# Sliding-window attention and a max-out feed-forward on one core: scores in 64x64 tiles for half of the chunks, masks as a minimum, and every slot written out by hand

## The chip, the cores and the metric

The kernel runs on one core of one Trainium2 chip. The metric is the device time of one execution in microseconds (us); lower is better. A profiled execution gives a page and a trace, in which each engine's instructions stand with their start and their duration: PE is TensorE's matmul, PEld its weight load, DVE VectorE, ACT ScalarE, POOL GpSimd, and SP the engine whose queue issues most of the DMAs.

## The reference

```python
# q, k, v: [4 batches, 8 heads, 768 positions, 64], float32; n_sink = 4, window = 128
scores = (q @ k.transpose(0, 1, 3, 2)) / 8
rel = pos[:, None] - pos[None, :]
keep = (pos[None, :] < n_sink) | ((rel >= 0) & (rel < window))
a = softmax(where(keep, scores, -1e9))
x = (a @ v).transpose(0, 2, 1, 3).reshape(3072, 512)
h = maximum(maximum(x @ w1, x @ w2), x @ w3)      # 512 -> 768
out = h @ w_out                                   # 768 -> 512
```

Each query sees the 128 keys up to its own position, and the first four keys of its batch (the sinks).

## The kernel before

The 3072 rows are cut into twelve **chunks** of 256 positions, three to a batch (`CPB` = 3). A chunk's positions are laid out with two neighbouring positions in one partition (`p i`, i = 0 or 1), so a chunk has two blocks n = 0, 1 of 128 positions, 64 partitions each. Four **pairs** p of heads (a = 0, 1: the heads of a pair, in partitions 0 to 63 and 64 to 127) go through the attention one by one.

For a chunk `ci` these steps are recorded, each a function of the kernel:

- `load`: three DMAs of 512 KB from SP's queue (q, k, v in float32, two buffers each). `cast_qk` makes bf16 halves of q and k, `cast_v` quarters of v, on the engine named in the call.
- `turn` (PE, chunks 0 to 3) or `turn_dma` (SP's queue, from chunk 4) turn q and k so that the head dimension lies in the partitions: one DMA transpose for q, two for k (one for each block of 64 partitions). `kT`, `qT` and `vb` are rings of four chunks.
- `score`: for each pair and head, the keys of a block are the stationary operand (64 rows, 128 columns) and the queries stream past. Block 0 of the chunk is multiplied with 256 queries, block 1 with 128, and block 1 of the chunk before with the first 128: 512 columns of moving data per head, in one PSUM bank `st`. The first chunk of a batch has no chunk before it: 384 columns.
- `expo`: ACT's exponential from PSUM into `e_sb` (bf16); `mask`: DVE multiplies `e_sb` with 0 or 1 (`msk`, `msk0`). In chunk 0 and a few pairs of chunk 1 a matmul adds the mask instead (`premask`).
- `sink_k`, `sink_v`, `sink_score`, `av_open`: the sinks' keys, values, scores, and their share of the output, in tiles of 32 columns or 32 rows of the array.
- `av`: e times v with a column of ones, then a reciprocal and a product on DVE into `x_sb`. `xpose` (PE) or, from chunk 4, `xpose_dma` (SP's queue) turns `x_sb` into `xT`.
- `ffn_h(ci, fp, wi)`: nine groups a chunk (three column pairs, three weights), each 8 matmuls of 256 columns into a bank `h_ps`; ACT copies the group of w1, DVE takes the maximum with the others. `ffn_y`: two groups a chunk of 6 matmuls with 512 columns; `store` writes 512 KB.

The program's order is the order in which these calls are written, engine by engine; nothing is rearranged after that, and each engine and queue works its list in order. Chunks 0 to 3 are written out call by call. From there a loop makes one **slot** per chunk, by five patterns: the slot of chunk n = i + 1 holds its attention, all of `ffn_h` of chunk i, and `ffn_y` of chunk i - 1. The slot of chunk n also loads, casts and turns chunk n + 2: the loads stand at its start, the DMA transposes at its end, `xpose_dma(n)` first, then k and q of chunk n + 2. The PSUM banks are handed out from a list of eight (`bank`, `give`).

Of the kernel before, what the change touches and what calls it, by code (L numbers as in the profile page):

```python
# [9 lines left out]
F32 = mybir.dt.float32  # L10
# [6 lines left out]
def kernel(  # L17
# [31 lines left out]
    with tc.manual_schedule():  # L49
# [17 lines left out]
        RING = 4  # L67
        kT = [const.tile([128, 2, NP, 2, 64], BF16, name=f"kT{i}") for i in range(RING)]
# [5 lines left out]
        raws, bfs = {}, {}  # L74

# [29 lines left out]
        def cast_v(ci, n, i, eng):  # L105
            if ci >= NCH:
                return
            eng.tensor_copy(  # L108
                vb[ci % RING][64 * i:64 * i + 64, n, :, 0:D],
                raws[ci, "v"][64 * n:64 * n + 64, :, i])  # L110

        def turn(ci, w, g, eng=None):

            pt = bank([128, 4, 128], BF16, "pt")
            x = bfs[ci, w]
            for i in range(4):
                y = x[:, 2 * g + i // 2, i % 2]
                nc.tensor.transpose(pt[:, i], y.rearrange("s a d -> s (a d)"), ident)  # L118
            eng = eng or (nc.scalar if w == "q" else nc.vector)
            f = eng.copy if eng is nc.scalar else eng.tensor_copy  # L120
            if w == "q":
# [31 lines left out]
        def turn_dma(ci, w):  # L153
# [7 lines left out]
            for n in range(2):  # L161
                nc.sync.dma_start_transpose(
                    out=kT[ci % RING][:, n].rearrange("q p i r -> q (p i) r"),
                    in_=bfs[ci, w][64 * n:64 * n + 64].rearrange("q p i a d -> q (p i a d)"))
# [51 lines left out]

        sel = const.tile([128, 2, 32], BF16, name="sel")
# [11 lines left out]
        def sink_k(b):  # L229
            x = kT[(b * CPB) % RING]  # L230
            for a in range(2):
                hp = slice(64 * a, 64 * a + 64)
                nc.gpsimd.tensor_copy(
                    ks[b % 2][hp, :, 4 * a:4 * a + 4].rearrange("q p (r i) -> q p r i", i=2),
                    x[hp, 0, :, :, 0:2].rearrange("q p i r -> q p r i"))
# [26 lines left out]

        def score(ci, pairs):
            b, c = divmod(ci, CPB)
# [28 lines left out]
        def mask(ci, p, eng=None):  # L293
            lo = 0 if ci % CPB else 1
            e = es[ci, p][0]
            (eng or nc.vector).tensor_mul(e[:, :, lo:], e[:, :, lo:], msk0 if lo else msk)  # L296
# [17 lines left out]
        def sink_v(b):  # L314
# [3 lines left out]
            for a in range(2):  # L318
                for p in range(NP):
                    nc.tensor.matmul(  # L320
                        sv[32 * p:32 * p + 32, a], lhsT=sel[:, a], rhs=x[:, 0, 2 * p + a],
# [137 lines left out]
        load(0, 'q', gate=pool_gate)  # L459
        masks()  # L460
        cast_qk(0, 'q', 1, nc.vector)
        warm(4)
        premask(0, (2,))
        premask(0, (0,))
        warm(9)
        cast_qk(0, 'k', 0, nc.scalar)
        turn(0, 'k', 0, nc.vector)
        load(0, 'v')
        cast_qk(0, 'q', 0, nc.scalar)
        turn(0, 'q', 1, nc.vector)  # L470
        sink_init()
        warm(1)
        cast_qk(0, 'k', 1, nc.gpsimd)
        cast_v(0, 1, 0, nc.vector)
        turn(0, 'k', 1, nc.scalar)
        load(1, 'k')
        turn(0, 'q', 0, nc.scalar)
        cast_v(0, 0, 1, nc.vector)
        score(0, (2,))
        masks_late()  # L480
        premask(0, (1,))
        load_w(0, 512, 768)
        load_w(0, 0, 512)
        cast_v(0, 0, 0, nc.vector)
        load(1, 'q')
        score(0, (0,))
        sink_k(0)
        expo(0, 2)
        load_w(1, 512, 768)
        cast_qk(1, 'k', 0, nc.vector)  # L490
        expo(0, 0)
        premask(0, (3,))
        cast_v(0, 1, 1, nc.vector)
        cast_qk(1, 'q', 0, nc.gpsimd)
        score(0, (1,))
        premask(1, (1,))
        turn2(1, 'k', 0, nc.vector)
        cast_qk(1, 'k', 1, nc.scalar)
        score(0, (3,))
        expo(0, 1)  # L500
        cast_qk(1, 'q', 1, nc.gpsimd)
        load(1, 'v')
        turn2(1, 'k', 1, nc.scalar)
        expo(0, 3)
        av_open(0)
        av(0, 0)
        av(0, 1)
        sink_v(0)
        turn2(1, 'q', 0, nc.vector)
        load_w(1, 0, 512)  # L510
# [12 lines left out]
        expo(1, 2)
        xpose(0, 1, nc.vector)
        xpose(0, 0, nc.vector)
        cast_v(1, 0, 0, nc.vector)
        premask(1, (3,))
        expo(1, 1)
        score(1, (3,))
        ffn_h(0, 2, 0)  # L530
        mask(1, 2)
        load(2, 'k', gate=after(0, 300))
        mask(1, 0)
        load_w(2, 512, 768)
        av_open(1)
        av(1, 2)
        av(1, 1)
        load_w(2, 0, 256)
        expo(1, 3)
        load(2, 'v', gate=after(1))  # L540
        av(1, 0)
        ffn_h(0, 1, 0)
        load(3, 'q', gate=after(0))
        av(1, 3)
        ffn_h(0, 0, 0)
        load_w(2, 256, 512)
        xpose(1, 1, nc.vector)
        xpose(1, 0, nc.scalar)
        ffn_h(0, 2, 1)
        cast_qk(2, 'q', 0, nc.gpsimd)  # L550
        load_wo(0, 3)
        ffn_h(1, 0, 0)
        ffn_h(1, 1, 0)
        load_wo(3, 6)
        ffn_h(1, 2, 0)
        load(3, 'k', gate=after(1))
        ffn_h(1, 0, 1)
        ffn_h(1, 1, 1)
        ffn_h(0, 0, 1)
        ffn_h(0, 1, 1)  # L560
        ffn_h(0, 2, 2)
        load(3, 'v', gate=after(2))
        cast_qk(2, 'k', 1, nc.scalar)
        cast_qk(2, 'k', 0, nc.gpsimd)
        cast_qk(2, 'q', 1, nc.vector)
        ffn_h(1, 2, 1)
        turn(2, 'q', 0, nc.scalar)
        ffn_h(1, 2, 2)
        turn(2, 'q', 1, nc.scalar)
        turn(2, 'k', 1, nc.vector)  # L570
        cast_v(2, 0, 1, nc.gpsimd)
        turn(2, 'k', 0, nc.vector)
        ffn_h(1, 0, 2)
        load(4, 'q')
        sink_score(2)
        score(2, (1,))
        load(4, 'k', gate=after(2))
        cast_v(2, 0, 0, nc.gpsimd)
        score(2, (2,))
        score(2, (3,))  # L580
        expo(2, 3)
        expo(2, 1)
        ffn_h(1, 1, 2)
        ffn_h(0, 0, 2)
        expo(2, 2)
        mask(2, 1)
        ffn_h(0, 1, 2)
        cast_v(2, 1, 1, nc.vector)
        cast_qk(3, 'q', 0, nc.gpsimd)
        cast_v(2, 1, 0, nc.vector)  # L590
        score(2, (0,))
        mask(2, 2)
        expo(2, 0)
        mask(2, 0)
        av_open(2)
        mask(2, 3)
        cast_qk(3, 'q', 1, nc.gpsimd)
        load(4, 'v', gate=pool_gate)
        ffn_y(1, 0)
        ffn_y(0, 0)  # L600
        cast_qk(3, 'k', 0, nc.scalar)
        av(2, 2)
        ffn_y(0, 1, nc.vector)
        av(2, 0)
        turn(3, 'q', 1, nc.scalar)
        turn(3, 'q', 0, nc.scalar)
        av(2, 3)
# [288 lines left out]
```

## Time and profile before

| | |
|---|---|
| median of three runs | 179.16 us (178.92 to 179.6) |
| the profiled execution | 179.04 us |
| its span in the trace | 177.3 us |
| PE busy | 170.1 us, 96% |
| DVE busy | 126.5 us, 71% |
| ACT busy | 85.8 us, 48% |
| POOL busy | 67.1 us, 38% |
| mean granted TensorE clock | 0.996 |

A row of a group on the page reads: line, engine, operation, what is written and read, shape and count, then the busy time, the mean duration of one in ns, and the idle time of the engine before them. A row of the timeline reads: start, length, engine, line, operation, and count; neighbours of one kind are merged. PE's matmuls overlap, so what one costs on PE is the distance from one start to the next, not the duration in its row.

### The profile page before, as it was taken

How to read it: one execution, taken by the hardware profiler on the slowest of the kernel's cores; microseconds unless marked ns; L12 is line 12 of the kernel's file. 1: busy time of each engine (PE TensorE's matmuls, PEld its weight loads, DVE VectorE, ACT ScalarE, POOL GpSimd, SP SyncE). 2: the span in 40 equal slices, each digit the busy share in tenths (PEclk: the TensorE clock that was granted, in tenths of full speed). 3: DMA queues.
4: the chain of work that ended last, by engine and by line, in shares of the span. 5: the costliest groups of instructions: out<-in, count | busy, mean ns of one | idle time of the engine just before them, and what ended most of it. 6: DMA issues, size and time to landing. Idle time of an engine off the chain costs nothing.

```text
span 177.3 us, 4632 instructions
## 1 busy us (share of the span) xinstructions
PE 170.1 (96%) x1872; PEld 127.1 (72%) x1872; DVE 126.5 (71%) x267; ACT 85.8 (48%) x171; POOL 67.1 (38%) x123
## 2 busy tenths in 40 slices
PE   6899999999998999999999999999999999999991
PEld 2446889856895597697696696796795895796870
DVE  3389738699698578796884984975885875966451
ACT  3498732577924822913724814814616617320210
POOL 6884344146580274544724624417427000000000
PEclk9999999999999999999999999999999999999998
DMA  5999999995999969999999999999999519305203
GB/s 141 290 287 203 224 248 259 216 265 148 290 140 236 94 142 299 129 245 173 251 269 189 210 301 160 213 303 153 198 293 198 150 34 379 125 11 170 120 0 118
DMA packets 69573, 34.90 MB, mean 197 GB/s; under 512 B 26544, under 2 KB 68016, under 8 KB 69552
## 3 DMA queue, kind: packets, MB, share of 16 engines
q1 hardware_dynamic: 64912, 31.33, 81.3%
q0 software_dynamic: 4496, 3.15, 11.6%
q8 instruction: 14, 0.23, 0.5%
q10 hardware_dynamic: 144, 0.13, 0.2%
q14 instruction: 7, 0.06, 0.1%
HBM read 25.17 MB, written 6.29 MB: 177 GB/s over the span
## 4 chain that ended last, share of the span: by engine, by line
PE 87%; DMA 4%; DVE 3%; SPq 2%; POOL 1%; ACT 1%; issue 0%; POOLq 0%
PE h_ps L394 52%; PE y_ps L415 18%; PE o L354 6%; PE st L278 6%; DMA q_raw<-in_q_dram 4%; SPq L90 2%; DVE h_sb L405 1%; PE o L336 1%; PE sk L304 1%; PE pt L118 1%; PE y_ps L425 1%; DVE x_sb L362 1%; POOL q_bf L102 1%; PE xt L375 1%; DVE vb L108 0%
## 5 line engine op out<-in xcount | busy, mean ns | idle before, releaser
L394 PE MATMUL h_ps<-xT,w 128*128 128x256 bf16 x864 | 100.7, 273 | 0.1
L394 PEld LDWEIGHTS <-w 128*128 128x128 bf16 x864 | 82.2, 98 | 10.4 <-issue 0.5
L405 DVE TENSOR_TENSOR h_sb<-h_sb,h_ps 128x512 bf16<-128x512 bf16 (+1 forms) x74 | 49.2, 671 | 21.2 <-PE h_ps L394 19.4
L290 ACT ACTIVATE e_sb<-st 128x512 bf16<-128x512 f32 (+1 forms) x96 | 46.6, 579 | 5.9 <-PE st L278 5.8
L401 ACT CAST h_sb<-h_ps 128x512 bf16<-128x512 f32 x36 | 21.2, 588 | 43.1 <-PE h_ps L394 42.9
L108 POOL CAST vb<-v_raw 64x512 bf16<-64x512 f32 x38 | 28.0, 737 | 15.8 <-DMA v_raw<-in_v_dram 14.5
L296 DVE TENSOR_TENSOR e_sb<-e_sb,msk 128x1024 bf16<-128x1024 bf16 (+1 forms) x42 | 31.6, 786 | 2.5 <-ACT e_sb L290 2.3
L415 PE MATMUL y_ps<-wo,h_sb 128*128 128x512 bf16 x138 | 32.4, 379 | 0.2 <-DVE h_sb L405 0.2
L415 PEld LDWEIGHTS <-h_sb 128*128 128x128 bf16 x138 | 12.6, 98 | 14.8 <-issue 1.6
L362 DVE TENSOR_TENSOR x_sb<-o,rc 128x256 bf16<-128x256 f32 x48 | 20.4, 425 | 1.6
L102 POOL CAST k_bf<-k_raw 128x512 bf16<-128x512 f32 x17 | 10.3, 625 | 28.5 <-DMA k_raw<-in_k_dram 28.5
L102 POOL CAST q_bf<-q_raw 128x512 bf16<-128x512 f32 x21 | 13.3, 658 | 16.4 <-DMA q_raw<-in_q_dram 13.0
L417 DVE COPY y_sb<-y_ps 128x512 f32<-128x512 f32 x13 | 9.0, 691 | 13.7 <-PE y_ps L415 13.7
L354 PE MATMUL o<-vb,e_sb 128*128 128x65 bf16 x352 | 16.5, 193 | 0.0
L354 PEld LDWEIGHTS <-e_sb 128*128 128x128 bf16 x352 | 14.6, 97 | 2.0 <-DVE e_sb L296 0.2
L278 PE MATMUL st<-qT,kT 64*128 64x128 bf16 (+1 forms) x256 | 14.5, 238 | 0.5 <-ACT kT L125 0.5
L278 PEld LDWEIGHTS <-kT 64*128 64x128 bf16 x256 | 8.1, 94 | 7.1 <-issue 4.9
L310 ACT ACTIVATE e_sink<-sk 128x256 bf16<-128x256 f32 x8 | 3.1, 385 | 14.8 <-PE sk L304 14.8
L359 DVE RECIPROCAL rc<-o 128x4 f32<-128x4 f32 x48 | 8.4, 175 | 1.3 <-PE o L354 1.0
L417 ACT COPY y_sb<-y_ps 128x512 f32<-128x512 f32 x10 | 5.9, 586 | 3.3 <-PE y_ps L415 2.7
L102 ACT CAST k_bf<-k_raw 128x512 bf16<-128x512 f32 x5 | 3.1, 626 | 6.5 <-DMA k_raw<-in_k_dram 6.5
L180 PE MATMUL warm<-wz 128*128 128x512 bf16 x14 | 4.5, 462 | 1.2 <-DVE wz L169 1.2
(69 smaller groups left out, 72.7 us busy)
## 6 DMA issues: line engine op xcount, KB each, us to landing
k_raw<-in_k_dram SPq DMA_DIRECT2D x12, 512.0 KB, 5.5
q_raw<-in_q_dram SPq DMA_DIRECT2D x12, 512.0 KB, 7.0
v_raw<-in_v_dram SPq DMA_DIRECT2D x12, 512.0 KB, 8.2
out_dram<-y_sb SPq DMA_DIRECT2D x11, 512.0 KB, 4.0
w<-in_moe_w_dram POOLq DMA_DIRECT2D x5, 256.0 KB, 8.7
w<-in_moe_w_dram POOLq DMA_DIRECT2D x2, 512.0 KB, 9.8
wo<-in_moe_w_out_dram POOLq DMA_DIRECT2D x2, 384.0 KB, 9.8
kT<-k_bf SPq DMA_TRANSPOSE x16, 3.7
```

The source lines that it names most:

```text
L102: f(x[:, 2 * g:2 * g + 2].rearrange("q p i a d -> q p a i d"), y[:, 4 * g:4 * g + 4].rearrange("q (p a) i d -> q p a i d", a=2))
L108: eng.tensor_copy(vb[ci % RING][64 * i:64 * i + 64, n, :, 0:D], raws[ci, "v"][64 * n:64 * n + 64, :, i])
L278: nc.tensor.matmul(st[a][:, s:s + q1 - q0].rearrange("q n (i r) -> q n i r", i=2), lhsT=x[hp, n, p].rearrange("q i r -> q (i r)"), rhs=qc[ ...
L290: nc.scalar.activation(e[:, a, lo:], st[a][:, lo:], AF.Exp, scale=scale)
L296: (eng or nc.vector).tensor_mul(e[:, :, lo:], e[:, :, lo:], msk0 if lo else msk)
L354: nc.tensor.matmul(o[:, t, a], lhsT=e[:, a, s], rhs=vb[cv % RING][:, n, 2 * p + a], start=first, stop=True, skip_group_check=True)
L362: nc.vector.tensor_mul(xs[ci][:, :, p], o[:, :, :, 0:D], rc.unsqueeze(3).to_broadcast([128, 2, 2, D]))
L394: nc.tensor.matmul(hp[:, f].rearrange("q (i t r) -> q i t r", i=2, t=2), lhsT=w_sb[wi][:, ds, c0:c0 + 128], rhs=xTs[ci][:, :, ds].rearrang ...
L401: nc.scalar.copy(dst, hp)
L405: nc.vector.tensor_max(dst[:, x], dst[:, x], hp[:, x])
L415: nc.tensor.matmul(yp, lhsT=hs[ci][:, fb, t * 128:(t + 1) * 128], rhs=wo[:, fb], start=(fb == 0), stop=(fb == FB - 1))
L417: (nc.scalar.copy if eng is None else eng.tensor_copy)(ys[ci][:, t], yp)
```

## The change

Seven things are done together.

1. **Scores of chunks 6 to 11** (`score_skew`; `SKEW` = 6). The 128 partitions of a chunk form four groups g of 64 keys (32 partitions, two positions each). A group sees only the 192 queries from its own position on. Each product is a tile of 64 rows and 64 columns of the array (`tile_position`), so that four tiles hold two heads and two key groups. A pair takes 16 matmuls, 8 with 128 columns and 8 with 64 (first chunks of a batch: 12 with 128), where it took 6 (4). Where a chunk has one before it, a quarter of each bank is not written and holds what was there.
2. **Masks** of these chunks are a minimum with 0 or the largest finite number (`mskg`, `mskg0`), because the unwritten part can hold anything; POOL makes them while chunk 1 is in work (`masks_skew`).
3. **K** of these chunks is turned by four DMA transposes of 32 partitions, not two of 64.
4. **V** of these chunks is cast by eight instructions of 32 partitions, not four of 64; its positions now follow the groups' order (`selg` for the sinks).
5. **PSUM banks** are eight tiles for the whole program, cut and bitcast for each use, not a new tile for each.
6. The **loop is gone**: every slot is a list of its own, and the order within it differs from chunk to chunk. Chunk n + 2 is still loaded, cast and turned in the slot of chunk n, but its k is turned ahead of `xpose_dma(n)` (chunks 8 to 10), not behind it; and `ffn_h` of chunk n - 1 goes on behind the last `av` of chunk n with fewer groups.
7. **Casts** of k and q move in part from POOL to DVE and ACT: on DVE 11 of k and 4 of q, where 2 and 2 were; on ACT 12 of q and 3 of k, where 1 and 5 were; on POOL 8 of q and 10 of k, where 21 and 17 were. The start (chunks 0 to 3) is written in another order as well; 13 warm-up matmuls, where 14 were.

The core of the diff:

```diff
+        BANK = [psum.tile([128, 512], F32, name=f"bank{j}") for j in range(8)]
         def bank(shape, dtype, name):
             j = free.pop(0)
-            x = psum.tile(shape, dtype, tag=f"b{j}", name=name)
+            x = BANK[j][:, 0:n] if dtype is F32 else BANK[j][:, 0:n // 2].bitcast(dtype)
...
+            for h in range(2):                       # cast_v from chunk 6
+                f(vb[ci % RING][64 * h + 32 * i:64 * h + 32 * i + 32, n, :, 0:D],
+                  raws[ci, "v"][64 * n + 32 * h:64 * n + 32 * h + 32, :, i])
...
+            for g in range(4):                       # turn_dma of k from chunk 6
+                nc.sync.dma_start_transpose(
+                    out=groups(ci)[:, :, g].rearrange("q p i r -> q (p i) r"),
+                    in_=bfs[ci, w][32 * g:32 * g + 32].rearrange("q p i a d -> q (p i a d)"))
...
+        def score_skew(ci, pairs):
+            k0, k1 = groups(ci - 1), groups(ci)
+            if ci % CPB:
+                plan = ((1, k1, 0, 0, None), (2, k1, 1, 1, None), (3, k1, 2, 1, None), (0, k0, 3, 0, None),
+                        (2, k1, 0, 1, 0), (1, k1, 1, 0, 1), (0, k0, 2, 0, 0), (3, k1, 3, 1, 1))
+            else:
+                plan = tuple((s, k1, g + h, t, None) for s, g, t in ((1, 0, 0), (2, 0, 1), (3, 2, 1)) for h in range(2))
+            for p in pairs:
+                st = [bank([128, 4, 128], F32, "st") for a in range(2)]
+                for s, x, g, t, u in plan:
+                    h = g % 2
+                    r = slice(0, 64) if u is None else slice(32 * u, 32 * u + 32)
+                    for a in range(2):
+                        hp = slice(64 * a, 64 * a + 64)
+                        nc.tensor.matmul(
+                            st[a][64 * h:64 * h + 64, s].rearrange("q (i r) -> q i r", i=2)[:, :, r],
+                            lhsT=x[hp, p, g].rearrange("q i r -> q (i r)"),
+                            rhs=qT[ci % RING][hp, p, :, t, r],
+                            start=True, stop=True, tile_position=(64 * a, 64 * h))
...
+            if ci >= SKEW:                           # mask
+                nc.vector.tensor_tensor(out=e[:, :, lo:], in0=e[:, :, lo:], in1=mskg0 if lo else mskg, op=ALU.min)
...
-        for i in range(3, NCH):
...
+        ffn_h(5, 0, 2)                               # from the slot of chunk 6
+        cast_qk(8, 'q', 0, nc.scalar)
+        xpose_dma(6)
+        turn_dma(8, 'q')
```

**PE, the first pair of chunk 7.** The rows are the weight loads and matmuls of one pair's scores; `kT_71` and `kT_79` are the chunk before, `kT_72` and `kT_80` this chunk. Before, the whole pair:

```order
L278 LDWEIGHTS kT_71
L278 MATMUL st<-qT_76,kT_71 128x128
L278 LDWEIGHTS kT_71
L278 MATMUL st<-qT_76,kT_71 128x128
L278 LDWEIGHTS kT_72
L278 MATMUL st<-qT_76,kT_72 128x256
L278 LDWEIGHTS kT_72
L278 MATMUL st<-qT_76,kT_72 128x256
L278 LDWEIGHTS kT_72
L278 MATMUL st<-qT_76,kT_72 128x128
L278 LDWEIGHTS kT_72
L278 MATMUL st<-qT_76,kT_72 128x128
```

Now, from the second half of a pair:

```order
L342 MATMUL bank_74<-qT_84,kT_80 64x2x32
L342 LDWEIGHTS kT_80
L342 MATMUL bank_76<-qT_84,kT_80 64x2x32
L342 LDWEIGHTS kT_79
L342 MATMUL bank_74<-qT_84,kT_79 64x2x32
L342 LDWEIGHTS kT_79
L342 MATMUL bank_76<-qT_84,kT_79 64x2x32
```

Six products that filled 128 partitions became 16 that fill 64; half of the 16 have 64 columns (2x32).

**SP, the slot of chunk 8.** The rows are DMAs in the order in which SP issues them, from `xpose_dma(7)` to `xpose_dma(8)`. Before, `kT_70` and `qT_74` are chunk 9's, the loads chunk 10's:

```order
L381 DMA_TRANSPOSE xT<-x_sb 128x8x128
L162 DMA_TRANSPOSE kT_70<-k_bf 128x8x64 x2
L157 DMA_TRANSPOSE qT_74<-q_bf 128x8x128
L431 DMA out_dram<-y_sb 128x1024
L90 DMA k_raw<-in_k_dram 128x8x128
L90 DMA q_raw<-in_q_dram 128x8x128
L90 DMA v_raw<-in_v_dram 128x8x128
L381 DMA_TRANSPOSE xT<-x_sb 128x8x128
```

Now, `qT_82` is chunk 9's, the loads and `kT_79`, `qT_83` are chunk 10's:

```order
L473 DMA_TRANSPOSE xT<-x_sb 128x8x128
L183 DMA_TRANSPOSE qT_82<-q_bf 128x8x128
L103 DMA k_raw<-in_k_dram 128x8x128
L103 DMA v_raw<-in_v_dram 128x8x128
L103 DMA q_raw<-in_q_dram 128x8x128
L523 DMA out_dram<-y_sb 128x1024
L194 DMA_TRANSPOSE kT_79<-k_bf 128x8x32 x4
L183 DMA_TRANSPOSE qT_83<-q_bf 128x8x128
L473 DMA_TRANSPOSE xT<-x_sb 128x8x128
```

Between two transposes of x, SP now has a load of k and the four transposes of that same k, and here two of q; before, the k that it turned there had been loaded ahead of the transpose of x with which the piece begins.

**DVE, the end of a chunk's attention.** The rows from the last two `x_sb` of a chunk to the first work of the next slot; `h_sb` rows take in feed-forward groups. Before (chunk 8; the `vs` row are the sinks of the next batch):

```order
L359 RECIPROCAL rc<-o 128x4
L362 TENSOR_TENSOR x_sb<-o,rc 128x2x128
L359 RECIPROCAL rc<-o 128x4
L362 TENSOR_TENSOR x_sb<-o,rc 128x2x128
L405 TENSOR_TENSOR h_sb<-h_sb,h_ps 128x512 x4
L323 CAST vs_84<-sv 128x130
L417 COPY y_sb<-y_ps 128x512
```

Now (chunk 8):

```order
L497 TENSOR_TENSOR h_sb<-h_sb,bank_74 128x512
L451 RECIPROCAL rc<-bank_72 128x4
L454 TENSOR_TENSOR x_sb<-bank_72,rc 128x2x128
L497 TENSOR_TENSOR h_sb<-h_sb,bank_76 128x512
L509 COPY y_sb<-bank_69 128x512
L386 TENSOR_TENSOR e_sb<-e_sb,mskg_111 128x2x384 x4
```

Where four feed-forward groups of the earlier chunk followed the last `x_sb`, one does now.

More of the change, by code (lines that the diff above doesn't have):

```diff
@@ L474 @@
[L474 to L478, printed above, removed]
-        score(0, (2,))
[L480 to L486, printed above, removed]
+        cast_qk(0, 'q', 0, nc.scalar)
+        warm(8)
+        turn(0, 'k', 0, nc.scalar)
+        load(1, 'k', gate=pool_gate)
@@ L538 @@
[L538 to L543, printed above, removed]
+        cast_v(1, 0, 0, nc.vector)
+        expo(1, 3)
+        ffn_h(0, 1, 0)
+        mask(1, 2)
+        load(2, 'v', gate=after(1))
+        load_w(2, 256, 512)
+        masks_skew(1)
+        av_open(1)
+        load(3, 'q', gate=after(0))
+        cast_qk(2, 'k', 1, nc.gpsimd)
+        load_wo(0, 3)
+        av(1, 0)
+        av(1, 1)
@@ L573 @@
[L573 to L591, printed above, removed]
```

874 lines of the change are left out of this document (554 added, 320 removed).

## The prediction

> **What bounds the kernel now.** The page's first lines come first, then the busy time in stretches of the span, because a share of the whole says nothing of a stage.
>
> ```profile
> PE 170.1 (96%) x1872; PEld 127.1 (72%) x1872; DVE 126.5 (71%) x267; ACT 85.8 (48%) x171; POOL 67.1 (38%) x123
> DMA  5999999995999969999999999999999519305203
> PE 87%; DMA 4%; DVE 3%; SPq 2%; POOL 1%; ACT 1%; issue 0%; POOLq 0%
> core 0: us, PE busy (x) PEld busy (x) DVE busy (x) ACT busy (x) POOL busy (x), PEclk, DMA share, GB/s
> 0.00:19.00 19.00, 16.36 (x184) 9.10 (x185) 12.27 (x39) 12.89 (x27) 12.28 (x35) 1.00 1.09 228
> 19.00:61.30 42.30, 41.52 (x468) 32.04 (x467) 31.18 (x65) 25.01 (x50) 17.33 (x33) 1.00 1.13 216
> 61.30:108.29 46.99, 46.99 (x536) 36.63 (x533) 36.84 (x73) 20.79 (x42) 23.34 (x35) 1.00 1.09 216
> 108.29:160.00 51.71, 51.71 (x587) 39.23 (x587) 38.31 (x78) 24.98 (x50) 14.19 (x24) 1.00 0.81 185
> ```
>
> PE has no idle time at all from 61.3 to 160 us, at a granted clock of 1.00, and 0.8 us of it from 19 to 61.3. What a change is worth is therefore what it takes from PE's own work, less every wait that it brings. The DMA engines are nearly as full until about 135 us (nines in the DMA row), so a transfer that comes later finds little room to catch up.
>
> The timeline of PE over chunk 8's slot (a chunk with one before it) and the start of chunk 9's (first of its batch) prices PE's work; distances between starts count, not the lengths.
>
> ```profile
> 108.29 0.29 PE L304 MATMUL sk<-qT,ks 128*32 128x256 bf16 x4
> 108.51 0.84 PE L278 MATMUL st<-qT,kT 64*128 64x128 bf16 x18
> 109.28 2.76 PE L415 MATMUL y_ps<-wo,h_sb 128*128 128x512 bf16 x12
> 111.98 0.39 PE L278 MATMUL st<-qT,kT 64*128 64x128 bf16 x6
> 112.30 0.29 PE L336 MATMUL o<-vs,e_sink 32*128 32x130 bf16 x8
> 112.53 0.42 PE L354 MATMUL o<-vb,e_sb 128*128 128x65 bf16 x8
> 112.78 1.91 PE L394 MATMUL h_ps<-xT,w 128*128 128x256 bf16 x16
> ...
> 117.00 4.53 PE L394 MATMUL h_ps<-xT,w 128*128 128x256 bf16 x40
> 121.46 0.25 PE L320 MATMUL sv<-vb,sel 128*32 128x65 bf16 x8
> 121.64 0.67 PE L278 MATMUL st<-qT,kT 64*128 64x256 bf16 x12
> 122.31 2.75 PE L415 MATMUL y_ps<-wo,h_sb 128*128 128x512 bf16 x12
> 124.99 0.34 PE L278 MATMUL st<-qT,kT 64*128 64x256 bf16 x4
> 125.26 0.35 PE L354 MATMUL o<-vb,e_sb 128*128 128x65 bf16 x6
> 125.45 0.82 PE L394 MATMUL h_ps<-xT,w 128*128 128x256 bf16 x6
> ```
>
> Three pairs of scores and one change of tile shape take 109.28 - 108.51 = 0.77 us, one pair and one change 0.32: a pair costs 0.225, a change of shape 0.095. In a first chunk 0.67 and 0.27 give 0.20 a pair. A feed-forward matmul takes (4.46 - 0.095) / 40 = 0.109 us, one of y 0.217, one of av 0.25 / 8 = 0.031. The last av of chunk 8 ends at 117.0, and its first feed-forward group (it needs `xT`) starts at 125.45: 8.4 us for the turn of x.
>
> **Scores: -0.9 us.** Two heads share the array now: 1024 columns in two tiles are 512 deep. The new pair has 8 x 128 + 8 x 64 = 1536 columns in four tiles, 384 deep: 0.225 x 384 / 512 = 0.169, saving 0.056 on each of 16 pairs (chunks 7, 8, 10, 11). First chunks (6, 9) have 12 x 128 / 4 = 384 columns, as before: nothing. That four tiles do run abreast is shown by the sinks' values: eight matmuls of 65 columns in four tiles take 121.64 - 121.46 - 0.095 = 0.085 us; one after the other, at 0.031, they would take 0.25. Bounds: the whole 0.9, or nothing, if a round of four with 64 columns lasts as long as one with 128 (four rounds of 0.056 are the old 0.225). I take the whole, since the row with 65 columns lies nearest. Changes of shape fall by one behind the first feed-forward group: -0.1.
>
> [...]
>
> **Four transposes of k, ahead of x: +1.7 us.** SP's queue over the same slot, from one transpose of x to the next, and the last rows with an idle queue:
>
> ```profile
> 105.47 2.17 SPq L381 DMA_TRANSPOSE xT<-x_sb  x1
> 107.75 2.52 SPq L162 DMA_TRANSPOSE kT<-k_bf  x2
> 110.36 1.26 SPq L157 DMA_TRANSPOSE qT<-q_bf  x1
> 111.71 0.53 SPq L431 DMA_DIRECT2D out_dram<-y_sb  x1
> 112.30 0.44 SPq L90 DMA_DIRECT2D k_raw<-in_k_dram  x1
> 112.79 1.26 SPq L90 DMA_DIRECT2D q_raw<-in_q_dram  x1
> 114.10 2.77 SPq L90 DMA_DIRECT2D v_raw<-in_v_dram  x1
> 118.64 1.79 SPq L381 DMA_TRANSPOSE xT<-x_sb  x1
> ...
> 144.31 1.24 SPq L381 DMA_TRANSPOSE xT<-x_sb  x1
> ```
>
> SP issues for 10.95 of these 13.17 us. A transpose costs 1.26 whether it has 64 partitions (k) or 128 (q, x), so I take 1.26 for 32 too; the other bound is half, 0.63. Two more a chunk are 2.5 us, more than the 2.2 that are free. Worse is the order: in chunks 8 to 10 k is loaded, cast and turned between two transposes of x, and the second x stands behind it. The rows for those steps (k's and x's landing where no store or load stands ahead, then the DVE and cast groups):
>
> ```profile
> DMA to landing us min/median/max: 4.6/4.6/4.6
> DMA to landing us min/median/max: 3.0/3.0/3.0
> L362 DVE TENSOR_TENSOR x_sb<-o,rc 128x256 bf16<-128x256 f32 x48 | 20.4, 425 | 1.6
> L102 POOL CAST k_bf<-k_raw 128x512 bf16<-128x512 f32 x17 | 10.3, 625 | 28.5 <-DMA k_raw<-in_k_dram 28.5
> L359 DVE RECIPROCAL rc<-o 128x4 f32<-128x4 f32 x48 | 8.4, 175 | 1.3 <-PE o L354 1.0
> L102 DVE CAST k_bf<-k_raw 128x512 bf16<-128x512 f32 x2 | 0.9, 428 | 0.2 <-DMA k_raw<-in_k_dram 0.2
> ```
>
> From one x to the next SP needs: x 1.3, k's load to landing 4.6, a cast 0.6 and about 0.5 until its engine is free, four transposes 5.1: 12.1 us with the gaps of 0.07. The new order puts no transpose of q between x of chunks 5 and 6, one between 6 and 7, two between 7 and 8: 12.1, 13.4, 14.8, together 40.3. PE's work from first feed-forward group to first feed-forward group, counted in the order at the prices above (72 matmuls of 0.109, two or three y groups of 1.3, av, 3 to 5 pairs, 2 to 8 changes), is 11.8, 13.5, 14.0: 39.3. So SP falls 1.0 us behind. Upper bound: where the DMA ring is full an issue takes 2.17, not 1.24; with 0.93 more in each of three slots, 3.8. I take 2.0, nearer the low end, because the loads have some 7 us to drain before these transposes.
>
> What cushions it is small. The new order leaves two h groups, two calls of scores with four changes and one y group between the last av of chunk 5 and its first feed-forward group: 1.75 + 0.65 + 0.4 + 1.3 = 4.1 us, where chunk 8 had 8.4. Reciprocal, product, issue and landing take 0.2 + 0.4 + 0.1 + 3.0 = 3.7. So 0.3 is covered, 1.7 left (0.7 to 3.5). Queued behind a late x on SP are q's transpose and the next load of k; waiting for it are PE's feed-forward groups, then everything. From chunk 9 on k's transposes stand behind x again, and I see no wait.
>
> **Casts, masks and banks: +0.5 us.** Eleven more casts of k and q go to DVE: 4.7 us more at 0.43, and a busier POOL beside them:
>
> ```profile
> L108 POOL CAST vb<-v_raw 64x512 bf16<-64x512 f32 x38 | 28.0, 737 | 15.8 <-DMA v_raw<-in_v_dram 14.5
> L296 DVE TENSOR_TENSOR e_sb<-e_sb,msk 128x1024 bf16<-128x1024 bf16 x30 | 23.3, 812 | 1.6 <-ACT e_sb L290 1.5
> L198 POOL TENSOR_SCALAR_AFFINE_SELECT addm<-addm 64x128 bf16<-64x128 bf16 x2 | 0.6, 295 | 0.1
> ```
>
> A v cast with 64 partitions (0.74) is no cheaper than a k cast with 128 (0.63), so I price one with 32 at 0.74; half is the other bound. Eight a chunk are 5.9 us of a slot's 12, hidden by two slots until they are used. The minimum has the product's shape: 0.81. DVE stays near 80% of a slot; what PE waits for late emptying is between 0 and 2 us, and I take 0.5, since before PE waited for nothing at 75%. The fixed banks change no work.
>
> **Start and end: +0.2 us.** Warm-up, scores and turns are written in another order, but the first feed-forward groups hang on the weights' landing in a full DMA (a 9 in every early slice). Eight selects of 0.3 and the copies of `masks_skew` keep POOL 3 us before its last weight loads. PE is idle 2.6 us before 19 and 0.8 before 61.3: I bound this by -1.5 and +1.5 and take 0. At the end `ffn_y(10, 1)` and its 512 KB store move next to the last stores: +0.2.
>
> **The sum.** -0.9 - 0.1 + 1.7 + 0.5 + 0.2 = +1.4 on the profiled execution's 179.04 us: 180.4. That execution lies 0.1 below the median of 179.16.
>
> **Rivals.**
> *Faster: SP keeps up.* If a transpose of 32 partitions issues in half the time, the three stretches are 9.6, 10.9 and 12.2, below PE's, and nothing waits: 179.04 - 1.0 + 0.2 = 178.2, with the start's bounds 176.9 to 178.9. It decides at 1.2 us a transpose (twelve of them, 0.7 us to lose). For it: so little is to lose. Against: 64 and 128 partitions cost the same.
> *The tiles don't run four abreast.* If each product starts 0.031 after the last, as in av, a pair takes 0.50 (a first chunk's 0.37): 16 x 0.27 + 8 x 0.17 = +5.7, and with 0.5 for the casts 185.2. [...]
> *DVE becomes the bound.* If its masks wait for the busier POOL, PE waits some 0.1 us at six emptyings in each of six slots: +3.6 beside the rest, 183.8. Against: DVE's 71%.
>
> **Chances.** Forecast 0.5, SP keeps up 0.32, DVE 0.12, no four abreast 0.06. The forecast's own range is 178.8 to 182.5. 176.9 to 183.9 leaves out the slow tiles and the tails. A measurement tells about 0.5% from no change, 178.3 to 180.1. Faster 0.27 (most of the second case), same 0.20 (its rest and 0.15 of the forecast), slower 0.53.
>
> **What would show it.** Right: a pair's scores at 0.17; SP's chain of k load, cast and four transposes of 1.26 ahead of x in chunks 8 to 10; PE waiting before the first `h_ps` of chunks 6, 7 and 8, about 2 us together. Wrong: no idle PE from 61 us on, transposes of 0.6, or a pair above 0.225; PE idle behind DVE names the third rival.

## The result and the profile after

The changed kernel takes 189.31 us (median of four, 186.32 to 190.25) against 179.06 before: slower, by a ratio of 1.0477, 95% interval 1.0386 to 1.0569. The ratios here and below are formed from the faster runs of a kernel alone, so where runs scatter, as these four do, the medians lie further apart (1.057 here). The forecast was 180.4, with 183.9 as its upper end. The profiled execution takes 189.01 us, its span is 187.3.

The page's first lines, and the busy time in the stretches used before (columns as there):

```profile
PE 169.0 (90%) x2076; PEld 127.0 (68%) x2095; DVE 127.0 (68%) x278; ACT 91.3 (49%) x183; POOL 73.9 (39%) x148
DMA  4999999989999939967996883999994744714006
PE 40%; DMA 33%; POOL 7%; SPq 6%; issue 5%; DVE 4%; ACT 1%; POOLq 0%; DVEq 0%; ACTq 0%
19.00:61.30 42.30, 41.64 (x491) 33.47 (x489) 32.21 (x71) 24.16 (x49) 23.10 (x46) 1.00 1.10 243
61.30:108.29 46.99, 42.12 (x538) 31.57 (x544) 31.57 (x68) 24.57 (x50) 17.57 (x34) 1.00 0.85 188
108.29:160.00 51.71, 46.39 (x676) 35.05 (x681) 35.23 (x77) 23.19 (x47) 18.85 (x33) 1.00 0.77 166
```

From 19 to 61.3 us PE is as busy as before. From there to 160 it stands still for 10.2 of 98.7 us, where it had no idle time; the clock stays at 1.00. The DMA row, nines before, has holes, and the DMA share falls from 1.09 and 0.81 to 0.85 and 0.77: the transfers became no heavier (34.9 MB in both), they start later. A third of the chain is DMA now. What PE waits for (total, times, longest; L486 is `ffn_h`, L507 `ffn_y`, L446 `av`, L367 the scores of the first six chunks):

```profile
PE bank L486 <- DMA xT<-x_sb: 6.6, 6, 1.7
PE bank L367 <- DMA qT<-q_bf: 1.7, 1, 1.7
PE bank L507 <- DVE h_sb L497: 0.7, 4, 0.3
PE bank L446 <- DVE e_sb L386: 0.7, 1, 0.7
```

Before, PE waited for no transpose at all. Now each of chunks 4 to 9 waits for its `xT`, 6.6 us in sum, and chunk 5's scores for `qT`: 8.3 of the 10 us by which the span grew. SP's queue over the slots of chunks 7 and 8 (L473 is x, L194 the four transposes of k, L183 q, L103 loads):

```profile
98.92 1.26 SPq L473 DMA_TRANSPOSE xT<-x_sb  x1
100.28 1.29 SPq L183 DMA_TRANSPOSE qT<-q_bf  x1
101.62 0.57 SPq L103 DMA_DIRECT2D k_raw<-in_k_dram  x1
...
103.39 1.62 SPq L103 DMA_DIRECT2D q_raw<-in_q_dram  x1
109.09 5.96 SPq L194 DMA_TRANSPOSE kT<-k_bf  x4
115.16 1.26 SPq L473 DMA_TRANSPOSE xT<-x_sb  x1
116.51 1.30 SPq L183 DMA_TRANSPOSE qT<-q_bf  x1
...
123.15 5.72 SPq L194 DMA_TRANSPOSE kT<-k_bf  x4
128.98 1.26 SPq L183 DMA_TRANSPOSE qT<-q_bf  x1
130.33 1.29 SPq L473 DMA_TRANSPOSE xT<-x_sb  x1
```

This is the chain that the prediction drew: from 105.0 to 109.09 the queue waits for k's load and cast, then come four transposes, then x (behind a transpose of q in chunk 8). From one x to the next it takes 16.2 and 15.2 us. PE at the end of chunk 8's slot:

```profile
129.00 0.70 PE L342 MATMUL bank<-qT,kT 64*64 64x128 bf16 x36
129.67 1.46 PE L507 MATMUL bank<-wo,h_sb 128*128 128x512 bf16 x5
131.05 0.36 PE L342 MATMUL bank<-qT,kT 64*64 64x128 bf16 x12
131.35 1.47 PE L507 MATMUL bank<-wo,h_sb 128*128 128x512 bf16 x6
134.52 1.70 PE L486 MATMUL bank<-xT,w 128*128 128x256 bf16 x14 [1.71 <-DMA xT<-x_sb]
```

After chunk 8's last av (128.0) PE has 4.8 us of other work, and x lands at 134.48.

### The profile page after: what moved, and what is told of

It reads as the page before. It is cut to its first block, busy times and chain, and to the rows that moved or that the text cites. A ratio compares the mean times of both kernels' runs of the same rounds, so it can differ in the third digit from the quotient of the medians.

```text
span 187.3 us, 5199 instructions
## 1 busy us (share of the span) xinstructions
PE 169.0 (90%) x2076; PEld 127.0 (68%) x2095; DVE 127.0 (68%) x278; ACT 91.3 (49%) x183; POOL 73.9 (39%) x148
## 4 chain that ended last, share of the span: by engine, by line
PE 40%; DMA 33%; POOL 7%; SPq 6%; issue 5%; DVE 4%; ACT 1%; POOLq 0%; DVEq 0%; ACTq 0%
PE bank L486 28%; DMA xT<-x_sb 10%; DMA q_raw<-in_q_dram 10%; DMA v_raw<-in_v_dram 8%; PE bank L507 6%; SPq L103 4%; DMA k_raw<-in_k_dram 3%; PE bank L446 3%; POOL vb L123 3%; POOL vb L127 2%; DVE h_sb L497 2%; DMA qT<-q_bf 1%; DVE x_sb L454 1%; ACT e_sb L379 1%; POOL q_bf L115 1%
## 5 line engine op out<-in xcount | busy, mean ns | idle before, releaser
L486 PE MATMUL bank<-xT,w 128*128 128x256 bf16 x864 | 101.0, 273 | 7.1 <-DMA xT<-x_sb 6.6
L486 PEld LDWEIGHTS <-w 128*128 128x128 bf16 x864 | 82.1, 98 | 20.5 <-DMA xT<-x_sb 6.5
L497 DVE TENSOR_TENSOR h_sb<-h_sb,bank 128x512 bf16<-128x512 bf16 (+1 forms) x74 | 48.6, 668 | 19.4 <-PE bank L486 16.3
L379 ACT ACTIVATE e_sb<-bank 128x512 bf16<-128x512 f32 (+1 forms) x96 | 46.7, 588 | 12.4 <-PE bank L367 7.6
L127 POOL CAST vb<-v_raw 32x512 bf16<-32x512 f32 x44 | 27.7, 630 | 28.7 <-DMA v_raw<-in_v_dram 23.8
L493 ACT CAST h_sb<-bank 128x512 bf16<-128x512 f32 x36 | 21.4, 607 | 26.1 <-PE bank L486 26.1
L507 PE MATMUL bank<-wo,h_sb 128*128 128x512 bf16 x120 | 31.7, 380 | 1.5 <-DVE h_sb L497 0.7
L454 DVE TENSOR_TENSOR x_sb<-bank,rc 128x256 bf16<-128x256 f32 x48 | 20.4, 424 | 1.6
L507 PEld LDWEIGHTS <-h_sb 128*128 128x128 bf16 x138 | 12.2, 98 | 12.9 <-DVE h_sb L497 1.0
L388 DVE TENSOR_TENSOR e_sb<-e_sb,msk 128x1024 bf16<-128x1024 bf16 (+1 forms) x18 | 13.3, 744 | 5.1 <-ACT e_sb L379 5.0
L446 PE MATMUL bank<-vb,e_sb 128*128 128x65 bf16 x352 | 15.3, 193 | 0.7 <-DVE e_sb L386 0.7
L446 PEld LDWEIGHTS <-e_sb 128*128 128x128 bf16 x352 | 13.6, 97 | 2.6 <-DVE e_sb L386 0.9
L123 POOL CAST vb<-v_raw 64x512 bf16<-64x512 f32 x15 | 10.7, 711 | 9.6 <-DMA v_raw<-in_v_dram 9.0
L402 ACT ACTIVATE e_sink<-bank 128x256 bf16<-128x256 f32 x8 | 3.3, 406 | 12.6 <-PE bank L396 8.0
L367 PE MATMUL bank<-qT,kT 64*128 64x128 bf16 (+1 forms) x128 | 7.5, 238 | 1.7 <-DMA qT<-q_bf 1.7
```

What stands on the lines that cost most here:

```text
L123: f(vb[ci % RING][64 * i:64 * i + 64, n, :, 0:D], raws[ci, "v"][64 * n:64 * n + 64, :, i])
L127: f(vb[ci % RING][64 * h + 32 * i:64 * h + 32 * i + 32, n, :, 0:D], raws[ci, "v"][64 * n + 32 * h:64 * n + 32 * h + 32, :, i])
L379: nc.scalar.activation(e[:, a, lo:], st[a][:, lo:], AF.Exp, scale=scale)
L446: nc.tensor.matmul(o[:, t, a], lhsT=e[:, a, s], rhs=vb[cv % RING][:, n, 2 * p + a], start=first, stop=True, skip_group_check=True)
L454: nc.vector.tensor_mul(xs[ci][:, :, p], o[:, :, :, 0:D], rc.unsqueeze(3).to_broadcast([128, 2, 2, D]))
L486: nc.tensor.matmul(hp[:, f].rearrange("q (i t r) -> q i t r", i=2, t=2), lhsT=w_sb[wi][:, ds, c0:c0 + 128], rhs=xTs[ci][:, :, ds].rearrang ...
```

## The experiments

The first theory was that the order of the calls costs the time (S), its rival that the pieces do (M). S fell with the first run; the two theories that followed, Q and F, are named where they come in.

**1. Old order, all pieces**: the start and the loop of before with the changed functions.

```diff
+        # start and loop as in the kernel before, at the end of the slot of chunk 4:
+                for part in range(3):
+                    masks_skew(part)
```

> The old order of calls (written-out start, loop, x turned ahead of k) with everything else of the change: 64x64 scores, minimum as mask, k in four transposes, v in eight casts, fixed banks. Theory S (the order of the new slots costs the time: x stands on SP behind k's load, cast and four transposes, and too little PE work lies between the last av and the first feed-forward group): the scores give 0.7 to 0.9 us, SP has 2.5 us more to issue per slot but behind x, so 178.0 to 180.5 us and no idle PE in front of h_ps. Rival M (the pieces themselves cost it: four transposes of 32 partitions and eight casts overload SP, the DMA ring and POOL wherever they stand): 184 us or more, with PE waiting for xT or qT/kT here too.

Measured: 191.86 us, 1.0687 (1.0664 to 1.0710). S falls: in the order of before, where x is turned ahead of k, the pieces cost 12.6 us, more than in the new one.

**2. New order, old pieces.**

```diff
-        SKEW = 2 * CPB
+        SKEW = NCH
```

> The new order of calls, but chunks 6 to 11 keep the old scores, the product as mask, two transposes of k and four casts of v (the two new masks are still made on POOL). Theory S: x still stands behind k's load and cast, but two transposes fewer a chunk take 2.5 us from each chain in slots 6 to 8 and 4, so 2 to 4 us of the 10 go: 185.5 to 188 with scores 0.8 dearer; waits for xT stay in chunks 4, 5 and 9. Rival M: 179 to 181, no waits for xT.

Measured: 180.64 us (179.58 to 183.92), 1.0069 (1.0036 to 1.0102), and no wait for `xT` above 0.2 us in its trace. The order alone costs 1.4 us; 8.7 are left for the pieces.

**3 and 4. x ahead of k, alone and with av earlier.** In the slots of chunks 4 to 8:

```diff
-        turn_dma(8, 'k')              # in front of the last av of chunk 6
...
         xpose_dma(6)
+        turn_dma(8, 'k')
         turn_dma(8, 'q')
...
-        ffn_h(5, 0, 1)                # run 4 alone: groups behind the last av
-        ffn_h(5, 1, 2)
         av(6, 3)
         av(6, 1)
+        ffn_h(5, 0, 1)
+        ffn_h(5, 1, 2)
```

> The changed kernel with one edit: in the slots of chunks 4 to 8 the transposes of k (and of q where it stood ahead) of chunk n + 2 are put on SP behind the transpose of x. Theory S, part 1 (SP's order alone): the waits for xT in chunks 5 to 8 go or shrink to the pure landing time of 3 to 4 us, 181 to 184 us. Part 2 (the short stretch of PE work between the last av and the first feed-forward group matters as much, since a landing takes 3 to 5 us even where the issue is prompt, as chunk 9 shows): 185 to 187. Rival M: 188 to 190, nothing changes.

> The edit of x first, and in the slots of chunks 4 to 9 the last av moved one or two feed-forward groups (0.9 to 1.8 us) earlier, so that 6 to 8 us of PE work lie between the last av and the first feed-forward group. Theory S: the waits for xT go, 179 to 181.5 us, with what the start (0.9) and DVE (1.5 to 2) cost left over. Rival M: 187 or more. A third outcome, 183 to 186, would say that av now waits for the masks instead (DVE).

Measured: 214.99 us (1.1961) and 208.34 (1.1622). Both theories missed. DVE in run 3, in the slot of chunk 6:

```profile
102.27 0.43 DVE L115 CAST k_bf<-k_raw 128x512 bf16<-128x512 f32 x1 [7.31 <-DMA k_raw<-in_k_dram]
102.61 0.17 DVE L451 RECIPROCAL rc<-bank 128x4 f32<-128x4 f32 x1
102.82 0.42 DVE L454 TENSOR_TENSOR x_sb<-bank,rc 128x256 bf16<-128x256 f32 x1
```

The k that is turned behind x pushes the next load of k back by its 5 us; the cast of that load stands on DVE's list ahead of the products of x, so DVE stands 7.3 us and x itself comes late. The new slots are written for a load that starts early, and x's place on SP cannot be changed by itself.

**5 to 8. Which piece.** Runs 5 and 6 take the extra transposes away and keep everything else (the right grouping of the keys is left out); runs 7 and 8 add the extra transposes to the order alone and to the kernel before (run 8 has the fixed banks too):

```diff
-            if ci < SKEW:             # turn_dma: two transposes of 64 for every chunk
+            if True:
...
-                            lhsT=x[hp, p, g].rearrange("q i r -> q (i r)"),
+                            lhsT=x[hp, g // 2, p, h],
...
             for g in range(4):        # runs 7 and 8, from chunk 6 on, old scores
+                    out=kT[ci % RING][:, g // 2, :, :, 32 * (g % 2):32 * (g % 2) + 32]...
```

> The changed kernel, but k of chunks 6 to 11 is turned by two transposes of 64 partitions, as before; the 64x64 tiles then take 64 neighbouring columns of that layout, so they multiply the wrong keys (this kernel leaves the right grouping of keys out). Scores' tiles, minimum, eight casts of v and the new order stay. Theory Q (the two more transposes of k a chunk cost it: each holds SP's queue for 1.25 us in which no load is started, and queue and DMA were already full): 179.5 to 181.5 us, near the 180.64 of the order alone less 0.8 for the scores. Rival P (the eight casts of v on POOL, the minimum or the small tiles cost it): 187 to 190.

> The same two transposes of k (wrong keys in the tiles, as in the run before) with the old order of calls, so all of the change but the transposes and the order. Theory Q: 178 to 179.5 us, what the scores save and little else. Rival P: 189 to 192, like the old order with four.

> The new order with the old scores, product as mask and four casts of v, and of the pieces only the four transposes of k in chunks 6 to 11 (they write the old layout). Theory Q: 187 to 190 us, 7 to 9 above the order alone. Rival P: 180 to 182.

> The kernel before with one edit: k of chunks 6 to 11 by four transposes of 32 partitions instead of two of 64, into the same layout. Theory Q: 2.5 us more on SP's queue in each of five slots, with nothing to take them up: 189 to 192 us. Rival P: 179 to 180.5.

| us, median | new order | old order |
|---|---|---|
| neither | 180.64 | 179.1 to 179.4 (before) |
| four transposes alone | 184.84 (1.0330; 1.0285 to 1.0375) | 187.67 (1.0488; 1.0438 to 1.0538) |
| the rest alone | 183.91 (1.0249; 1.0204 to 1.0294) | 182.40, 179.05 to 184.47 (1.0037; 0.9990 to 1.0085) |
| both | 189.31 | 191.86 |

Theory Q (the two more transposes, which the queue has no room for) holds for the larger part: two more transposes a chunk cost 4.2 us in the new order and 8.3 in the old. But in the new order the rest costs 3.3 us as well, where up to about 1 less was expected. In the old order no cost of the rest is shown: its median lies 3 us higher, but its ten runs reach from 179.05 to 184.47, and the ratio's interval includes 1. SP's queue in run 8, one slot:

```profile
109.14 3.25 SPq L473 DMA_TRANSPOSE xT<-x_sb  x1
112.49 5.91 SPq L194 DMA_TRANSPOSE kT<-k_bf  x4
118.50 1.25 SPq L183 DMA_TRANSPOSE qT<-q_bf  x1
119.85 0.52 SPq L523 DMA_DIRECT2D out_dram<-y_sb  x1
120.42 0.43 SPq L103 DMA_DIRECT2D k_raw<-in_k_dram  x1
120.91 1.07 SPq L103 DMA_DIRECT2D q_raw<-in_q_dram  x1
122.02 1.49 SPq L103 DMA_DIRECT2D v_raw<-in_v_dram  x1
123.62 3.30 SPq L473 DMA_TRANSPOSE xT<-x_sb  x1
```

There is no pause in it, and a slot lasts 14.5 us where PE needs 13.2. The landings tell the two phases of a slot: in the slot that begins at 94.28, q's transpose lands at 106.97, then store, k, q and v at 108.83, 110.90, 112.70 and 114.41, so 2 MB in 7.4 us, and x 0.9 later. During the loads SP is held (x's issue takes 3.25 us while three loads ahead of it have not landed). During the transposes, 1.3 apart, hardly anything else moves: 43 GB/s from 101.61 to 105.10, against 270 from 106.97 to 114.41. So in this slot the two phases add.

**9 and 10. Two of k's four transposes on ACT's queue**, with before's scores and with all pieces, in the old order.

```diff
-                turn_dma(i + 3, 'k')
+                turn_dma(i + 3, 'k', nc.sync, (0, 1))
+                turn_dma(i + 3, 'k', nc.scalar, (2, 3))
```

> The kernel before with four transposes of k in chunks 6 to 11 (187.67 us when SP issues all), of which ACT's queue now issues two, behind its last copy of a slot, where ACT is idle. Theory Q1 (the time that a transpose holds SP's queue is what costs it): SP is back at two transposes of k a slot, 179 to 180.5 us. Rival Q2 (the DMA engines work off transposes one after the other wherever they are issued, or small transposes cost them more): 185 to 188.

> Everything of the change with the old order of calls (191.86 us), two of k's four transposes on ACT's queue. Theory Q1: 178.3 to 181 us, depending on what the eight casts of v cost POOL. Rival Q2: 189 to 192.

Measured: 223.46 us (1.2469) and 221.79 (1.2389). They do not tell Q1 from Q2: the program makes transposes of the two queues wait for each other's landing (ACT issues at 88.31, lands at 90.62; SP issues at 90.63, lands at 92.94; ACT at 92.97), 2.3 us each, and ACT's exponentials stand behind that:

```profile
88.31 5.84 ACTq L194 DMA_TRANSPOSE kT<-k_bf  x2
94.28 0.87 ACT L379 ACTIVATE e_sb<-bank 128x384 bf16<-128x384 f32 x2 [11.83 <-issue]
```

**11 and 12. The casts of v**: run 5 with four casts of v instead of eight, and the order alone with eight instead of four.

```diff
-            if ci < SKEW:             # cast_v: 64 partitions
+            if True:                  # run 11
+            if ci < 2 * CPB:          # run 12
```

> The changed kernel with two transposes of k and four casts of v from chunk 6 on (keys and values in the wrong order in the tiles; the right grouping is left out): of the pieces the 64x64 tiles, the minimum and the fixed banks are left. With eight casts of v it took 183.91, the order alone 180.64. If the casts of v cost the difference (POOL's list makes k's casts later, and SP's transposes with them): 179 to 181. If the tiles or the minimum cost it: 183 to 185.

> The new order alone (180.64 us) with v of chunks 6 to 11 cast by eight instructions of 32 partitions (v's positions then do not fit the old scores' order; the right order is left out). If the casts of v cost it: 183 to 185. If not: 180 to 181.5.

Measured: 183.94 us (1.0277; 1.0237 to 1.0317) and 183.32 (1.0227; 1.0194 to 1.0260). Neither cause fits both runs: without the eight casts the 3 us stay, and with them alone 2.7 come too (its runs, 182.57 to 186.03, overlap those of the order alone, 179.58 to 183.92). Either two costs hide behind one another, or something other than the pieces' work makes the difference; these two runs do not tell which. In the trace of run 11 the queue is empty when x of chunk 9 is issued at 137.46, and still:

```profile
L473 SPq DMA_TRANSPOSE xT<-x_sb x1: 1233/1233/1233, 137.5 to 137.5; - x1
DMA to landing us min/median/max: 4.9/4.9/4.9
```

where 3.1 is usual. The packet records show why: a packet of 16 KB of the queue that the page calls q8 instruction starts at 140.4 and takes 0.93 us. Of the 32 packets of 4 bytes that close x, 30 start by 140.1, and the last two at 141.3, when that packet has ended. Over all profiles but those of runs 9 and 10, counting transposes with nothing earlier left in the queue when their issue ended:

| transpose | no such packet in the 2.0 us (k: 1.2) from the issue's end | with one |
|---|---|---|
| x, issue's end to landing, median | 1.84 us (63) | 3.39 us (13) |
| k | 1.11 us (77) | 2.63 us (15) |

The packets come on average about every 120 matmuls of PE's program (with 120 weight loads), 14 in the kernel before and 16 now.

**13 to 15. PE's program moved by 40 matmuls** against everything else:

```diff
-        warm(8)
+        warm_small(48)                # 32 columns stationary, 64 moving
```

> The changed kernel with two transposes of k (183.91 us; keys wrong in the tiles), with one edit: at the start 48 small warm-up matmuls (32 columns stationary, 64 moving) stand for the 8 of 512 columns, so that everything after them lies 40 matmuls later in PE's program. Theory F (16 KB packets of the instruction queue, one for about every 120 matmuls of PE's program, delay a DMA transpose that they meet by about 1.6 us; here they meet x of chunks 8 and 9 and k in front of x of chunk 7): the packets now fall some 3 to 4 us earlier in each slot, beside x: 181 to 182.3 us. Rival V (tiles, minimum or casts of v cost the 3 us): 183.5 to 184.5.

> The same 48 small matmuls in the new order alone (180.64 us), where the packets met the turn of q and not that of x in chunk 9. Theory F: the shift brings them onto x of chunks 7 and 9: 182.5 to 184.5 us. Rival V: 180 to 181.5.

> The same 48 small matmuls in the changed kernel itself (189.31 us). The packets met k or q ahead of x of chunks 4, 5, 7 and 8, and x of chunk 9. Theory F: with twelve to fourteen of these transposes ahead of x the packets meet some others; only chunk 9's x (1.6 us) is surely freed: 186.5 to 189. Rival V: 189 to 190.

Measured: 182.29 us (1.0192; 1.0139 to 1.0245), 181.09 (1.0092; 1.0061 to 1.0122) and 188.17 (1.0531; 1.0485 to 1.0577). What PE waits for in run 5, and then in run 13:

```profile
PE bank L486 <- DMA xT<-x_sb: 2.6, 3, 1.2
```

```profile
PE bank L493 <- DMA xT<-x_sb: 2.1, 1, 2.1
```

Run 13 is as expected by its median (the runs overlap: 181.77 to 183.94 against 182.63 to 184.93 in run 5), and its trace tells more. In run 5 x of chunks 8 and 9 lands 4.6 us after its issue; in run 13 it takes 3.1 and 3.2, and chunks 7, 8 and 9 no longer wait. One packet, at 97.0, now meets x of chunk 6, which lands after 4.6 us and makes PE wait 2.1 us. The packets moved and the stalls with them. Run 14 missed: in its trace they met the transposes of q at 109.42 and 120.08, not x as I had worked out, and the time stayed within its spread. Run 15's 1.1 us lie inside the forecast of theory F, and also near the spread of the kernel.

**16. Loads of q and v on ACT's queue**, all pieces, old order.

```diff
-                    nc.sync.dma_start(
+                    (nc.scalar if ci >= 2 * CPB and w in "qv" else nc.sync).dma_start(
```

> All pieces of the change in the old order of calls (191.86 us; four transposes of k, right keys), with the loads of q and v of chunks 6 to 11 issued from ACT's queue instead of SP's. Theory Q1 (SP's queue is the bound: while it issues a transpose, 1.25 us each, no load starts): 178.5 to 182 us. Rival Q2 (the DMA engines are the bound, or ACT waits too long for its issues): 187 to 193.

Measured: 186.23 us, 1.0386 (1.0357 to 1.0415): 5.6 of the 12.6 us come back, between the two theories. SP is freed, and PE's waits for x fall from 9.2 us to 1.2, but ACT pays: between its load of q at 93.94 and that of v at 98.02 it issues nothing, the exponentials stand behind, and PE waits 3.5 us for ACT.

**17 and 18. Slack or proportion, total or latency.** The kernel before with three transposes of k, and with four and the load of v moved behind them.

```diff
+            # run 17: block 0 by one transpose of 64 partitions, then
-            for g in range(4):
+            for g in (2, 3):
...
-                load(i + 3)           # run 18
+                load(i + 3, 'kq')
...
                 turn_dma(i + 3, 'q')
+                load(i + 3, 'v')
```

> The kernel before with three transposes of k in chunks 6 to 11 (one of 64 partitions, two of 32) where it had two and where four took 187.67 us. Theory Q1 (the queue of SP is a serial resource with a slack of about 1.8 us a slot, in which it waits for x): one more transpose, 1.25 us, fits into the slack, 179 to 180.5 us. Rival Q2 (each transpose costs in proportion, by the load on the DMA engines): half of the loss of four, 182.5 to 184.

> The kernel before with four transposes of k (187.67 us), and in the slots of chunks 5 to 10 the load of v moved behind the transposes of x, k and q, with its casts; so x stands behind two loads in the ring instead of three. Theory T (the queue's total per slot is the bound, in whatever order): 186 to 189 us. Rival L (only x's landing behind the loads is): x lands 1.7 us earlier in each slot, 181 to 184.

Measured: 183.26 us (1.0222; 1.0159 to 1.0284) and 194.82 (1.0825; 1.0739 to 1.0910). One more transpose a chunk costs 3.9 us, two 8.3 (PE's waits for x are 2.8 and 6.0 us): in proportion, as Q2 had it, with no sign of the slack of Q1. In six chunks these are 7.5 and 15 us of SP's issue, so about half of it shows. Run 18 does not decide between T and L. PE's waits for x are all but gone, 0.3 us, as L would have it; but the edit brought new ones, 4.7 us for `ks` and 3.6 us for `vb`, which POOL now makes late, and the kernel is 7 us slower. No kernel's median is below that of the kernel before.

## Why the prediction was wrong, step by step

**Right.** Slower, by SP's chain of k load, cast, four transposes and x. A transpose of 32 partitions holds SP as long (median 1.24 us) as one of 64 or 128 (1.26), so the rival by which SP keeps up had no ground. The waits stand at the first `h_ps` of chunks 6, 7 and 8, among others, but these three are 4.3 us, where about 2 were forecast. A cast of v with 32 partitions is hardly cheaper than one with 64 (0.63 us against 0.71 in the same trace), and the minimum is cheaper than the product (0.70 us at 128x1024, against 0.74 in the same trace and 0.81 in the trace before):

```profile
L127 POOL CAST vb<-v_raw 32x512 bf16<-32x512 f32 x44 | 27.7, 630 | 28.7 <-DMA v_raw<-in_v_dram 23.8
L386 DVE TENSOR_TENSOR e_sb<-e_sb,mskg 128x1024 bf16<-128x1024 bf16 (+1 forms) x24 | 15.0, 649 | 4.4 <-ACT e_sb L379 4.2
```

DVE did not become the bound (68%; PE's waits for its `h_sb` and `e_sb` are 1.8 us, where 0.5 was taken and 2 was the bound). The tiles do run abreast: a pair's 16 matmuls take 0.19 us (the scores, below), where 16 at av's distance of 0.031 would take 0.50. The third rival's time should read 184.0 (180.4 + 3.6), not 183.8; nothing hangs on it.

**The step that failed: "+1.7" for the transposes of k.** By the medians the two more transposes alone cost 4.2 (order alone against order with four) to 5.4 us (run 5 against the changed kernel). PE's waits for x and q, which the term stands for, are 8.3 us; 2.6 us of waits for x are left in run 5 without the extra transposes. Three things in the term were wrong.

*The places.* The sum let x be late in chunks 6, 7 and 8, since it took k to be turned ahead of x for chunks 8 to 10 only. The k of chunks 6 and 7 stands ahead of x of chunks 4 and 5 in the same way, and I passed over it. From the end of x's product to its issue the queue took 3.4, 1.1, 1.7, 0.9 and 0.7 us in chunks 4 to 8.

*The lengths.* For the three chains 12.1, 13.4 and 14.8 us were counted, 40.3; they take 13.6, 16.2 and 15.2, 45.0. The four transposes of k take 5.7 to 6.6 instead of 5.1, since single issues take 2.1 and 2.7 where 1.2 is usual (for its own long issue, 2.17 us, the prediction names a full ring; the row shows the length alone), and the load of k with its cast up to 7.5 (101.62 to 109.09) instead of 5.7. Against PE's 39.3 this is 5.7 behind, not 1.0.

*The slack.* "More than the 2.2 that are free" took SP's waiting for x as free time. It is not: in that time the queue still moves the loads (v, issued at 114.10 in the trace before, lands at 122.53). Run 17 shows it: the transpose that should have fitted costs 3.9 us.

**"From chunk 9 on I see no wait".** Chunk 9 waits 1.1 us. Its x is issued 0.06 us after the product and lands 4.8 later; a packet of the instruction queue starts in between, at 145.1. The prediction set 3.7 us for the turn of x against 4.1 us of PE work. That 3.7 rests on a landing of 3.0, which about every sixth x does not keep (13 of the 76 in the table).

**Scores, -0.9.** Two pairs of chunk 8 and one change of shape:

```profile
114.57 0.54 PE L342 MATMUL bank<-qT,kT 64*64 64x128 bf16 x32
115.05 0.39 PE L507 MATMUL bank<-wo,h_sb 128*128 128x512 bf16 x1
```

(115.05 - 114.57 - 0.095) / 2 = 0.19 us: a pair takes 0.19 instead of 0.225, not 0.169, and 16 x 0.035 = 0.6. A weight load of 64 columns (`L342`) lasts 107 ns in this trace, one of 128 columns (`L278`) 94 ns in the trace before, both medians; whether these loads take a part of the gain was not shown.

**Casts +0.5, start and end +0.2.** The order alone, with the moved casts, costs 1.4; the changed kernel's first feed-forward matmul stands at 17.56 us, 0.9 later than before (16.68).

**A second miss, as large.** The other pieces (tiles, minimum, casts of v, banks) were put at about -0.5 (-0.9, -0.1, +0.5). In the new order they cost 3.3 (run 5 against run 2) to 4.5 us (run 7 against the changed kernel).

Not settled: how these 3 us and more divide between stalls by instruction packets and work. Run 13 gives the first about 1.6 by the medians, and in run 5 PE waits 1.1 us for a mask. Whether SP's issue or the DMA engines' handling of transposes is the harder limit stays open too, since run 16 moved part of the wait to ACT.

## What to carry to other kernels

Where a DMA queue has no pause, price a transfer by what the queue then has in a period, against PE's period (14.5 against 13.2 us in run 8), and don't count as free the time in which the issuing engine waits: the queue may still be draining (the transpose that run 17 set against 1.8 us of SP's waiting cost 3.9). Look up every place where a moved transfer now stands ahead of another one, chunk by chunk. Work that covers just the median landing is too little: in the kernel before x of chunks 4 to 9 landed 4.3 to 5.8 us after its issue, and still 0.4 to 2.9 us before PE came to its feed-forward groups.

## What the runs showed of the hardware

**Instruction packets.** A transpose of x or k into which a 16 KB packet of q8 instruction falls lands 1.5 us later (medians of the table: 3.39 against 1.84 us, 2.63 against 1.11). From one packet to the next PE works off about 120 matmuls and their weight loads on average. That such a packet delays a transfer, and so that the length of PE's program moves stalls about (runs 5 and 13), I had not expected.

**The clock after a short stop.** In run 17 PE stands still for 2.3 us ahead of 128.3, and its clock falls (columns as in the stretches, PEclk the third from the end):

```profile
128.30:130.00 1.70, 1.70 (x9) 1.21 (x9) 0.00 (x0) 0.00 (x0) 1.28 (x4) 0.50 0.49 93
130.00:132.00 2.00, 2.00 (x17) 1.55 (x16) 0.01 (x1) 0.78 (x2) 0.00 (x0) 0.62 1.13 302
132.00:134.00 2.00, 2.00 (x29) 1.83 (x27) 1.48 (x4) 0.39 (x1) 0.00 (x0) 1.00 0.91 211
```

From these clocks an estimate: that stop cost some 1.6 us more (half of 1.7, 0.38 of 2.0). In run 13 a stop of 2.1 us is followed by 1.00, and so are those of the changed kernel, none over 1.8. The length alone does not decide: in run 18 a stop of 2.3 us is followed by a mean clock of 0.54, and one of 2.4 us by 1.00 (the stop is the first row of each two):

```profile
95.35:97.64 2.29, 0.00 (x1) 0.00 (x1) 0.69 (x1) 0.00 (x0) 2.06 (x5) 1.00 1.22 297
97.64:101.38 3.74, 3.52 (x27) 1.81 (x29) 0.00 (x0) 3.27 (x7) 2.34 (x4) 0.54 0.80 85
144.96:147.33 2.37, 0.00 (x1) 0.00 (x1) 0.69 (x1) 0.00 (x0) 2.14 (x5) 1.00 1.16 307
147.33:150.00 2.67, 2.62 (x29) 1.49 (x31) 0.17 (x1) 2.32 (x6) 2.15 (x4) 1.00 0.97 198
```

In the old order the stops are longer: 3.9 us in run 8, then 3.0 us at 0.50; 5.8 and 3.1 us in run 1, then 4.4 us at 0.50 and 4.0 us at 0.57. From these figures an estimate: about 1.5 of run 8's 8.3 us and 3.9 of run 1's 12.6 are the slower clock, not the waits themselves.

**Transposes by DMA.** Four of 32 partitions move as much as two of 64, 256 KB, and take the queue twice as long (5.1 us and more against 2.5); the loads beside them move 2 MB in 7.4 us.
